# Another order of the first block's lists, and a query bound's small operations behind its maximum, in an attention and GEGLU block on one core

## The chip, the cores and the metric

The kernel runs on one core of a Trainium2 chip. The metric is the device time of one execution in microseconds (us), taken as the median of several runs. PE is the matrix engine (PEld its weight loads), ACT is ScalarE, DVE is VectorE, POOL is GpSimd and SP is SyncE, which issues most DMAs.

## The reference

One transformer block for a prompt of 2048 tokens of width 512, in float32: attention with 32 query heads of 16 columns that share one key and one value head, and then a GEGLU feed-forward of inner width 1792.

```python
def _A_ref(x, wq, wk, wv, wo):      # H = 32, Dh = 16
    q = (x @ wq).reshape(B, S, H, Dh).transpose(0, 2, 1, 3)
    k = x @ wk
    v = x @ wv
    scores = jnp.einsum("bhqd,bkd->bhqk", q, k) * (Dh ** -0.5)
    p = _softmax(scores, axis=-1)
    o = jnp.einsum("bhqk,bkd->bhqd", p, v)
    return o.transpose(0, 2, 1, 3).reshape(B, S, H * Dh) @ wo
def _B_ref(x, w_gate, w_up, w_down):
    return (_gelu(x @ w_gate) * (x @ w_up)) @ w_down
h = x + _A_ref(_layernorm(x), ...)
h2 = h + _B_ref(_layernorm(h), ...)
```

## The kernel before

The queries are cut into four blocks of 512 tokens. A block has eight groups of four heads, and a group runs over 16 chunks of 128 keys. The unit of attention is a *score pair* (`scores`, L352 and L356): two matmuls that write a PSUM tile of 128 keys x 1024, and one exponential of ScalarE over it into the tile p. Two pairs make a chunk; its V-product (`weigh`, L360) is a set of matmuls that add p's four heads into the accumulator acc. In the first block there are three PSUM tiles for score pairs (s twice, s3 once), one bank for the accumulator and one bank, "d", for everything else. A block has 256 pairs, counted here from 0, and 128 V-products.

A group's last V-product is followed by `evacuate`: DVE copies acc to oT (L373), SyncE writes oT to DRAM (`acc_d`, L374), and a later step reads it back turned (oc, four DMAs, L384). After every second group DVE takes reciprocals of the sums (L389), multiplies and splits the result into o_hi and o_lo. For the last group of block 0 all these steps are emitted at once. The first dense product, `project` (pp, L761), reads o_hi and o_lo.

A float32 product is made of three products of rounded parts, "hi" and "lo", so operands are split: `split` makes a rounded copy (L125) and the rest (L126).

The softmax needs no maxima: a bound of each query's scores, from the norms of q and k, is subtracted, as one more row of q. `project_q` makes the queries of a block in four column parts: twelve matmuls each into bank d (L205), the split, the squares qs, and three DMAs into `q_d`. Behind the four parts a small matmul adds the squares up by head (pqn, L243), DVE copies the result to qn (L247) and takes its maximum (L248), GpSimd makes scale and shift of it in four operations on 32 x 1 elements (mm, L252 to L259), DVE makes the row m (L270), and SyncE stores it (L272). The first column part of block 0 is made in the prologue with a bound of its own ("urgent"); the other three parts of block 0 and all of blocks 1 to 3 are made within the first block, as one generator, `later_q`. Its last step, `check_bound`, takes the largest bound and writes it to `b_d` with a DMA (L1363) from the tile q2m. `project_q` yields a number after each step, by which the caller counts.

The order in the first block is written out by hand as two lists of letters, `OPENING` once and `PERIOD` eight times (for eight groups). The letter s calls `pace`: one score pair, and after every fourth pair a step of turned outputs (`take_out`) and one part of the dense weights. The letter v is one V-product, p is a `visit` of the query generator, and n is `norm`, which runs the sums of squares if the last visit ended with a 4. A visit takes steps until their numbers add up to 6, or until a 2 comes. After the lists the pairs go on in a simple loop to pair 278, and then the woven lists of the dense phase begin.

The dense weights are split on GpSimd during the first block: `part_weights` has 46 parts, each a load, the split into a hi and a lo tile, and a store to DRAM (w_d, L460 and L466). At the end of the block the tiles of the queries and of these parts are given up (`early.close()`), and the tiles of the dense phase take their memory. `prime` issues the first nine loads into these: three of x (L519), three of the first weights (L501) and three of the second (L509). Where it stands is said by a count of pairs in `pace`:

```python
if n == 2 * PER:
    drain()
    ...
    early.close()
    db = late.enter_context(tc.tile_pool(name="dense", bufs=1))
...
score(n)
n += 1
...
if n == 2 * PER + 4:
    prime()
```

`PER` is 128. PE, ACT and POOL run in the order of emission in all of the attention, and SP and DVE do so in the first block's lists and the loops after it.

Of the kernel before, what the change touches and what calls it, by code (L numbers as in the profile page):

```python
# [29 lines left out]

HURRY = ((0, 3), (1, 0), (1, 1))

OPENING = "ssspsspsp"

PERIOD = "ssvssvssvnssvvsssvsvssvssvvssspssvvsssvvsspsssvvsnssp"

RUNS = ((0, 1, 2, 3), (4, 5, 6, 7), (8, 9, 10, 11), (12, 13))

# [19 lines left out]
def kernel(  # L58
# [62 lines left out]
    def split(eng_hi, hi, lo, src, eng_lo=None):  # L121
        if eng_hi is nc.scalar:
            nc.scalar.activation(hi, src, AF.Copy)
        else:
            eng_hi.tensor_copy(hi, src)  # L125
        (eng_lo or nc.vector).tensor_tensor(lo, src, hi.bitcast(F32), op=ALU.subtract)  # L126
# [29 lines left out]
    def run(outer, first):  # L156
# [10 lines left out]
        def psum1(name):  # L167
            if not spare:
                return ps.tile([P, T], F32, tag="d", bufs=width, name=name)
            tag, bank = take_bank(name)  # L170
            spare.append(tag)
            return bank
# [22 lines left out]
        def project_q(b, cs, eng, col):  # L195
            tsl = slice(b * T, (b + 1) * T)
            xT_hi, xT_lo = xT[b]
            urgent = b == 0 and cs[0] == 0
            qss = []
            for c in cs:  # L200
                pq = psum1(f"pq_{b}_{c}")
                n = 0
                for d in range(DC):
                    for wt, xt in ((wq_hi, xT_hi), (wq_hi, xT_lo), (wq_lo, xT_hi)):
                        nc.tensor.matmul(  # L205
                            pq, wt[:, d, c * P : (c + 1) * P], xt[:, d, :],
                            start=(n == 0), stop=(n == 3 * DC - 1),
                        )
                        n += 1
                    if urgent or d < DC - 1:  # L210
                        yield 3

                raw = None
                if (b, c) in HURRY:
                    raw = eb.tile([P, T], F32, tag="vT", bufs=3, name=f"pq_raw_{b}_{c}")
                    if b == 0:
                        nc.scalar.activation(raw, pq, AF.Copy)
                    else:
                        nc.vector.tensor_copy(raw, pq)
                    yield 3  # L220
                qh = eb.tile([P, T], F32R, tag="qh", bufs=2, name=f"qh_{b}_{c}")
                ql = eb.tile([P, T], F32R, tag="ql", bufs=2, name=f"ql_{b}_{c}")
                if raw is not None:
                    split(nc.vector, qh, ql, raw)
                else:

                    split(nc.vector if b == 0 and c == FIRST_Q else eng, qh, ql, pq)
                qs = eb.tile([P, T], BF16, tag="qs", bufs=DC, name=f"qs_{b}_{c}")
                (nc.gpsimd if urgent else nc.vector).tensor_tensor(
                    qs, qh.bitcast(F32), qh.bitcast(F32), op=ALU.mult  # L230
                )
                qss.append(qs)
                for r0, part in ((0, qh), (DH, ql), (2 * DH, qh)):
                    nc.sync.dma_start(
                        q_d[c * HC : (c + 1) * HC, r0 : r0 + DH, tsl].bitcast(F32),
                        part.bitcast(F32),
                    )
                if raw is None or b == 0:
                    yield 4 if b > 0 and c == DC - 1 else 3

            pn = psum1(f"pqn_{b}_{cs[0]}")[:H, :]
            for i, c in enumerate(cs):
                nc.tensor.matmul(  # L243
                    pn, sel[:, c, :], qss[i], start=(i == 0), stop=(i == len(cs) - 1)
                )
            qn = eb.tile([H, T], F32, tag="qn", bufs=1, name=f"qn_{b}_{cs[0]}")
            nc.vector.tensor_copy(qn, pn)  # L247
            nc.vector.tensor_reduce(q2[:, col : col + 1], qn, axis=AX.X, op=ALU.max)  # L248
            yield 2

            mm = eb.tile([H, 3], F32, tag="mm", bufs=2, name=f"mm_{b}_{cs[0]}")
            nc.gpsimd.tensor_scalar(  # L252
                mm[:, 0:1], q2[:, col : col + 1], k2m, 1e-30, op0=ALU.mult, op1=ALU.add
            )
            nc.gpsimd.tensor_tensor(mm[:, 1:2], mm[:, 0:1], power[:H, 0:1], op=ALU.pow)
            nc.gpsimd.tensor_scalar(
                mm[:, 2:3], mm[:, 0:1], mm[:, 1:2], 0.5, op0=ALU.mult, op1=ALU.mult
            )
            nc.gpsimd.tensor_scalar(  # L259
                mm[:, 1:2], mm[:, 1:2], k2m, 0.5, op0=ALU.mult, op1=ALU.mult  # L260
            )
            m = eb.tile([H, T], F32R, tag="m", bufs=2, name=f"m_{b}_{cs[0]}")
            if urgent:
                nc.scalar.activation(
                    m, qn, AF.Identity, bias=mm[:, 2:3], scale=mm[:, 1:2]
                )
                ms[b] = m
                return
            yield 0
            nc.vector.tensor_scalar(m, qn, mm[:, 1:2], mm[:, 2:3], op0=ALU.mult, op1=ALU.add)  # L270
            hs = slice(cs[0] * HC, (cs[-1] + 1) * HC)
            nc.sync.dma_start(q_d[hs, 3 * DH, tsl].bitcast(F32), m[hs].bitcast(F32))  # L272
            yield 2

        ms = {}
        q_first = project_q(0, range(FIRST_Q), nc.scalar, 0)
# [2 lines left out]
        def later_q():  # L279
            second = project_q(1, range(DC), nc.vector, 1)  # L280
            for _ in range(DC):
                yield next(second)

            next(q_rest)
            yield from q_rest
            yield from second
            for b in range(2, NB):
                yield from project_q(b, range(DC), nc.vector, b)
            check_bound(eb, k2m)
# [77 lines left out]
        def take_out():  # L367
            for step in outs.pop(0):
                step()
# [162 lines left out]
        def prime():  # L532
            new_xT(0)
            for i in range(3):
                load_x(i)
                load_w1(i)
            for j in range(3):
                load_w2(0, j)
# [405 lines left out]
        work = None  # L944
# [11 lines left out]
        def drain():  # L956
            nonlocal work
            for _ in work or ():
                pass
            work = None  # L960
# [30 lines left out]
        with tc.manual_schedule(engines={mybir.EngineType.SP, mybir.EngineType.DVE}):  # L991
            parts = None
            if first:
                work = later_q()
                parts = part_weights(early.enter_context(tc.tile_pool(name="parts", bufs=1)))


            normed = True

            def visit():  # L1000
                nonlocal work, normed
                total, k = 0, None
                while work is not None and total < 6 and (k != 2 or last == 0):
                    last, k = k, next(work, None)
                    if k is None:
                        work = None
                        return
                    total += k
                normed = k != 4

            def norm():
                nonlocal normed
                if not normed:
                    next(work)
                    normed = True

            def pace():
                nonlocal n, parts, db, tiny
                if n == 2 * PER:
                    drain()  # L1020
                    for _ in parts or ():
                        pass
                    parts = None
                    early.close()
                    db = late.enter_context(tc.tile_pool(name="dense", bufs=1))
                    tiny = late.enter_context(tc.tile_pool(name="tiny", bufs=1))
                score(n)
                n += 1
                if n % 4:
                    return  # L1030
                if outs:
                    take_out()
                if parts is not None and n > 12 and n % 24:
                    next(parts, None)
                if n == 2 * PER + 4:
                    prime()

            moves = {"s": pace, "p": visit, "n": norm, "v": partial(finish, 1)}
            for move in OPENING + PERIOD * (PER // KC):
                moves[move]()  # L1040
            while n < lead:
                pace()
                if n % 4 == 2 and len(pend) > 2 and n < lead - 1:
                    finish(1)
                elif n % 4 == 0:
                    finish(len(pend) - 2)
# [394 lines left out]
```

## Time and profile before

| | us |
|---|---|
| median of 3 runs | 1422.35 |
| lowest and highest | 1422.34, 1423.45 |
| the profiled execution | 1423.57 |
| its span, first to last instruction | 1421.5 |

The profiled execution lies about 2 us above its span and 1.2 us above the median. Its mean granted clock of TensorE was 0.995. Times within the profile count from the start of the span; the lists of the first block run from about 52 to 310 us. In a timeline's row stand the start, the length, the engine and line, the operation with its tiles, the count of merged instructions, and in brackets the idle time before it and what ended it. "SPq" is SyncE's queue.

### The profile page before, as it was taken

The numbers are of one execution on the slowest core, as the hardware profiler recorded it, in microseconds if no ns is written. First come the engines' busy times: TensorE is split into PE (matmuls) and PEld (weight loads), VectorE is DVE, ScalarE is ACT, GpSimd is POOL, SyncE is SP. The second block draws the span as 40 slices with busy tenths as digits, with TensorE's granted clock in tenths as the row PEclk, the third lists the DMA queues.
The fourth block names the chain that finished last, engine by engine and source line by source line (L and its number), as shares of the span: only waits on it lengthen the run. The fifth ranks groups of instructions, "written<-read, shape, count | busy, mean of one in ns | idle before, by whom it ended". The sixth has DMA issues, their size and how long they took to land.

```text
span 1421.5 us, 25079 instructions
## 1 busy us (share of the span) xinstructions
PE 1392.2 (98%) x10384; PEld 752.6 (53%) x10384; DVE 635.9 (45%) x1043; ACT 1030.0 (72%) x1147; POOL 217.0 (15%) x305
## 2 busy tenths in 40 slices
PE   6999999999999999999999999999999999999998
PEld 5433333335455555555555555545555555557886
DVE  7413121314364354454354444445354453437665
ACT  6699999997777777777777777777777777752000
POOL 5586776610000000000000000000000000001000
PEclk9999999999999999999999999999999999999999
DMA  4467666625222333322432333311332332244452
GB/s 158 138 200 247 211 222 212 222 98 201 73 88 94 116 101 116 101 65 57 156 102 86 127 105 101 104 61 42 141 105 90 116 116 101 90 148 174 126 189 77
DMA packets 66930, 180.57 MB, mean 127 GB/s; under 512 B 9436, under 2 KB 9436, under 8 KB 66776
## 3 DMA queue, kind: packets, MB, share of 16 engines
q1 hardware_dynamic: 56976, 144.79, 30.8%
q0 software_dynamic: 9760, 34.08, 7.3%
q8 instruction: 84, 1.38, 0.4%
q14 instruction: 38, 0.31, 0.1%
q10 hardware_dynamic: 72, 0.00, 0.0%
HBM read 131.13 MB, written 47.71 MB: 126 GB/s over the span
## 4 chain that ended last, share of the span: by engine, by line
PE 93%; ACT 2%; DVE 2%; DMA 1%; issue 1%; POOL 0%; SPq 0%; DVEq 0%; ACTq 0%; POOLq 0%
PE acc L360 32%; PE s L352 20%; PE pg L761 8%; PE pu L761 8%; PE pd L761 8%; PE pq L205 3%; PE pd L791 3%; PE pp L761 3%; PE pu L791 2%; PE pg L791 2%; ACT p L356 2%; PE pd_rest L803 1%; PE pxt L587 0%; DMA w<-w_d 0%; PE pk L1229 0%
## 5 line engine op out<-in xcount | busy, mean ns | idle before, releaser
L356 ACT ACTIVATE p<-s 128x1024 f32<-128x1024 f32 x1024 | 959.5, 1040 | 233.8 <-PE s L352 233.5
L360 PE MATMUL acc<-p,v_sb 128*32 128x512 f32 x4096 | 491.7, 600 | 0.0
L352 PE MATMUL s<-qg,kaug 50*128 50x512 f32 x1984 | 386.5, 426 | 4.0 <-ACT p L356 3.5
L352 PEld LDWEIGHTS s<-qg,kaug 50*128 50x128 f32 x1984 | 170.7, 184 | 288.2 <-issue 131.3
L360 PEld LDWEIGHTS acc<-p,v_sb 128*32 128x32 f32 x4096 | 110.4, 109 | 229.6 <-issue 216.1
L761 PE MATMUL pg<-x2h,w 64*128 64x512 f32 x672 | 173.9, 392 | 0.0
L761 PE MATMUL pu<-x2h,w 64*128 64x512 f32 x672 | 172.5, 391 | 0.0
L135 POOL TENSOR_SCALAR rstd<-mv 128x1 f32<-128x1 f32 x16 | 3.5, 220 | 968.0 <-DVE mv L133 967.8
L761 PE MATMUL pd<-w,gh 64*128 64x512 f32 x624 | 123.9, 392 | 1.4 <-DVE h L691 1.4
L691 DVE TENSOR_TENSOR h<-h,pd 128x512 f32<-128x512 f32 x80 | 54.4, 686 | 148.1 <-PE pd L761 148.1
L761 PEld LDWEIGHTS pg<-x2h,w 64*128 64x128 f32 x672 | 94.3, 185 | 11.5
L761 PEld LDWEIGHTS pu<-x2h,w 64*128 64x128 f32 x672 | 94.2, 185 | 11.5
L761 PE MATMUL pg<-x2l,w 64*128 64x512 f32 x336 | 99.2, 391 | 0.0
L761 PE MATMUL pu<-x2l,w 64*128 64x512 f32 x336 | 98.8, 391 | 0.0
L761 PEld LDWEIGHTS pd<-w,gh 64*128 64x128 f32 x624 | 68.3, 185 | 13.3 <-DVE h L691 2.7
L900 ACT ACTIVATE ga<-ga 128x512 f32<-128x512 f32 x14 | 8.8, 632 | 91.0 <-DVE ga L897 91.0
L389 DVE RECIPROCAL oc<-oc 128x128 f32<-128x128 f32 x64 | 56.6, 922 | 37.4 <-DMA oc<-acc_d 37.3
L761 PE MATMUL pd<-w,gl 64*128 64x512 f32 x312 | 71.7, 391 | 0.0
L628 DVE TENSOR_TENSOR g<-g,pg 128x512 f32<-128x512 f32 x42 | 28.8, 685 | 90.5 <-PE pg L761 90.5
L624 DVE COPY g<-pg 128x512 f32<-128x512 f32 x42 | 29.1, 692 | 72.1 <-PE pg L761 72.1
L628 DVE TENSOR_TENSOR u<-u,pu 128x512 f32<-128x512 f32 x42 | 28.8, 686 | 68.0 <-PE pu L761 68.0
L125 DVE CAST qh<-pq 128x512 fp32r<-128x512 f32 x11 | 7.6, 690 | 113.3 <-PE pq L205 113.3
(244 smaller groups left out, 1478.9 us busy)
## 6 DMA issues: line engine op xcount, KB each, us to landing
w<-w_d SPq DMA_DIRECT2D x112, 512.0 KB
w<-w_d SPq DMA_DIRECT2D x28, 1024.0 KB
qg<-q_d SPq DMA_DIRECT2D x62, 200.0 KB
q_d<-qh SPq DMA_DIRECT2D x32, 256.0 KB
acc_d<-oT SPq DMA_DIRECT2D x32, 256.0 KB
oc<-acc_d SPq DMA_DIRECT2D x128, 64.0 KB
w_d<-w_0b POOLq DMA_DIRECT2D x14, 512.0 KB, 4.1
w_d<-w_1b POOLq DMA_DIRECT2D x14, 512.0 KB, 3.8
```

The costliest lines, as they stand in the source:

```text
L205: nc.tensor.matmul(pq, wt[:, d, c * P : (c + 1) * P], xt[:, d, :], start=(n == 0), stop=(n == 3 * DC - 1),)
L352: nc.tensor.matmul(s[:, a, :], kaug[rows, kc * P : (kc + 1) * P], qg[rows, u, :], start=True, stop=True,)
L356: nc.scalar.activation(p[:, 2 * u : 2 * u + 2, :], s, AF.Exp, scale=SCALE)
L360: nc.tensor.matmul(acc[32 * j : 32 * j + 32, :], v_sb[:, kc, :], p[:, j, :], start=(kc == 0), stop=(kc == KC - 1), skip_group_check=True,)
L389: nc.vector.reciprocal(oc[:, 1, sl], oc[:, 1, sl])
L624: nc.vector.tensor_copy(half, bank)
L628: nc.vector.tensor_tensor(half, half, bank, op=ALU.add)
L691: nc.vector.tensor_tensor(hs[b, t], hs[b, t], bank, op=ALU.add)
L761: nc.tensor.matmul(bank, lhsT[r], rhs[r], start=(k == 0), stop=(k == n - 1), skip_group_check=True,)
L791: nc.tensor.matmul(bank, lhsT, rhs, start=(i == 0), stop=(i == len(ts) - 1))
L803: nc.tensor.matmul(bank, lhsT, rhs, start=(i == 0), stop=(i == len(ts) - 1))
L900: nc.scalar.activation(a, a, AF.Tanh, scale=GELU_A * GELU_C)
```

## The change

Three things are changed. `OPENING` and `PERIOD` get another order. For the queries other than the urgent ones, the yield of 2 that stood between the maximum and the four GpSimd operations moves behind these; the yield of 0 that stood ahead of m is gone, and the yield of 2 behind m's DMA is now 0. So the four operations are emitted in the same visit as the maximum, and m and its DMA remain at the start of the next visit. And `visit` no longer goes on behind a 2 that follows a 0: it ends at every 2.

```diff
-OPENING = "ssspsspsp"
-
-PERIOD = "ssvssvssvnssvvsssvsvssvssvvssspssvvsssvvsspsssvvsnssp"
+OPENING = "ssspssps"
+
+PERIOD = "psssvvssvnsspsssvvssvnssvssvssvvssspssvssvvnsssvvssvss"
...
             nc.vector.tensor_reduce(q2[:, col : col + 1], qn, axis=AX.X, op=ALU.max)
-            yield 2
-
+            if urgent:
+                yield 2
             mm = eb.tile([H, 3], F32, tag="mm", bufs=2, name=f"mm_{b}_{cs[0]}")
             nc.gpsimd.tensor_scalar(
                 mm[:, 0:1], q2[:, col : col + 1], k2m, 1e-30, op0=ALU.mult, op1=ALU.add
...
                 ms[b] = m
                 return
-            yield 0
+            yield 2
             nc.vector.tensor_scalar(m, qn, mm[:, 1:2], mm[:, 2:3], op0=ALU.mult, op1=ALU.add)
             hs = slice(cs[0] * HC, (cs[-1] + 1) * HC)
             nc.sync.dma_start(q_d[hs, 3 * DH, tsl].bitcast(F32), m[hs].bitcast(F32))
-            yield 2
+            yield 0
...
                 total, k = 0, None
-                while work is not None and total < 6 and (k != 2 or last == 0):
-                    last, k = k, next(work, None)
+                while work is not None and total < 6 and k != 2:
+                    k = next(work, None)
                     if k is None:
                         work = None
                         return
```

## The prediction

> **What bounds the kernel now.** I read the page first, then the chain of waits in the first block, then the timelines of PE, GpSimd, SyncE and DVE around the places where the two lists differ.
>
> ```profile
> span 1421.5 us, 25079 instructions
> PE 1392.2 (98%) x10384; PEld 752.6 (53%) x10384; DVE 635.9 (45%) x1043; ACT 1030.0 (72%) x1147; POOL 217.0 (15%) x305
> PE 93%; ACT 2%; DVE 2%; DMA 1%; issue 1%; POOL 0%; SPq 0%; DVEq 0%; ACTq 0%; POOLq 0%
> ```
>
> The chain that ends last is 93% PE: a microsecond in which PE stands still anywhere is, to within little, a microsecond of the kernel. The next view is the chain of waits from 68 to 300 us (the first block's lists) and some of its pieces from 151 to 184 us (start, length, engine, line, matmul records); the last row is one of ScalarE's timeline.
>
> ```profile
> by line: PE acc L360 48.7%; PE s L352 33.8%; PE pq L205 15.1%; ACT p L356 1.0%; PE pqn L243 0.8%; issue 0.4%; DVE qn L247 0.3%; ACTq L356 0.0%
> ...
> 162.11 1.85 PE acc L360 x16
> 163.97 0.89 PE s L352 x6
> 164.86 0.99 PE acc L360 x8
> ...
> 172.49 1.59 PE pq L205 x6
> 174.08 0.66 PE s L352 x3
> ...
> 71.25 7.44 ACT L356 ACTIVATE p<-s 128x1024 f32<-128x1024 f32 x8 [0.45 <-PE s L352]
> ```
>
> So the first block too is PE's: only 1.0 + 0.4 + 0.3 = 1.7% of 232 us, 3.9 us, is time in which PE waited. The pieces give prices: two V-products in a row 1.85, a single one 0.99, a run of three score pairs 0.89 and of two 0.66 (0.20 a run and 0.23 a pair), a projection visit of six matmuls 1.59. ScalarE takes (7.44 - 1.10) / 7 = 0.906 us a pair, the last one's 1.10 taken off.
>
> **The order of the lists.** I counted the letters of both periods. Each has 32 s, 16 v and 3 p, and, what matters for PE, the same runs: 14 of s, 11 of v (5 doubles, 6 singles), 3 of p. PE's own time in a period is 14 x 0.20 + 32 x 0.23 + 5 x 1.85 + 6 x 0.99 + 3 x 1.59 = 30.1 us in both, against 32 x 0.906 = 29.0 for ScalarE. The order can therefore give back only PE's waits, at most 3.9 us. The old gaps between visits are 19, 7 and 6 pairs, the new ones 7, 14 and 11. In a gap PE gains 0.906 - (0.66 + 0.99) / 2 = 0.08 us a pair on ScalarE and can spend it only as far as the three score tiles reach; 19 pairs gain 1.5, 14 pairs 1.1. I take a gain of 1.4 us (0.2 a period over seven full ones), between -1 (the product of block 1's squares is now followed by a projection after two pairs, as block 2's was) and 3.9. Opening, drain and the pairs after the lists stay as they were.
>
> **The small operations.** Four GpSimd operations (L252 to L259) now stand one visit earlier, behind their maximum; m on DVE and its DMA stay in the next visit. GpSimd runs its queue in order, and that queue is otherwise the splitting of the dense weights, 46 parts that wait for nothing in the attention. So a bound set early in that queue stops the splitting until DVE has the maximum. Here is GpSimd's timeline where the bound of block 1, of block 2 and of block 3 stand or will stand, with DVE's maximum of block 1 ahead:
>
> ```profile
> 131.41 0.67 DVE L248 TENSOR_REDUCE q<-qn 32x1 f32<-32x512 f32 x1
> ...
> 111.47 1.28 POOL L126 TENSOR_TENSOR w_1b<-w_1r,w_1b 128x512 fp32r<-128x512 f32 x1
> ...
> 132.00 1.28 POOL L126 TENSOR_TENSOR w23b<-w23r,w23b 128x512 fp32r<-128x512 f32 x1
> ...
> 134.94 0.74 POOL L466 DMA_DIRECT2D w_d<-w23b  x1
> ...
> 202.82 1.28 POOL L126 TENSOR_TENSOR w_1b<-w_1r,w_1b 128x512 fp32r<-128x512 f32 x1
> ...
> 211.66 1.28 POOL L126 TENSOR_TENSOR w_0b<-w_0r,w_0b 128x512 fp32r<-128x512 f32 x1
> ...
> 220.32 0.64 POOL L460 DMA_DIRECT2D w_d<-w_0b  x1 [0.63 <-issue]
> ...
> 291.39 0.63 POOL L466 DMA_DIRECT2D w_d<-w213b  x1 [0.30 <-POOL w213b L126]
> 306.84 0.25 POOL L252 TENSOR_SCALAR mm<-q,k2m 32x1 f32<-32x1 f32 x1 [14.83 <-DVE q L248]
> ```
>
> By the lists, block 1's bound moves from behind part 16 (w23b, done at 133.28) to behind part 12 (w_1b, done at 112.75). Its maximum ends at 132.08 now; in the new list it comes one pair earlier and about 1 us of order gain sooner, 130.8. So GpSimd stands still from 113 to 130.8, and the chain of four takes 1.6: 132.4. (The first bound, which now also stands ahead of the first weight loads, delays the first parts by some us; this stand swallows it.) Then parts 13 to 16 (112.75 to 133.28: 20.5), 17 to 30 (134.64 to 204.10: 69.5), block 2's bound now behind part 30 and no longer behind part 32 (1.6, its maximum long there), parts 31 and 32 (204.10 to 212.94: 8.8) and the rest (220.0 to 292.0: 72.0): 132.4 + 20.5 + 69.5 + 1.6 + 8.8 + 72.0 = 304.8. In those stretches are data waits of up to 5 us each that may fall differently; I take 303, between 299 and 308, where it is 292.0 now. DVE's m of block 2 then waits until about 224; behind it on DVE stands the split of the projection at pair 172 (about 219.5), whose bank PE needs again only at pair 186: free. On SyncE m's DMA holds back a turn of outputs that is not due before pair 220: free.
>
> **What the shifted end does.** In both kernels the dense phase's first nine loads (`prime`) are issued in the pace of pair 259, and the last group of block 0 is evacuated at V-product 127. In the old list that product stands between pairs 258 and 259, in the new one behind 259. SyncE keeps program order, so the nine loads now go ahead of the write and the turn of the last outputs. Today's rows, SyncE, then DVE, then PE:
>
> ```profile
> 309.05 0.35 SPq L272 DMA_DIRECT2D q_d<-m  x1
> 309.50 0.36 SPq L1363 DMA_DIRECT2D b_d<-q2m  x1
> 309.95 0.38 SPq L374 DMA_DIRECT2D acc_d<-oT  x1
> 316.86 1.92 SPq L384 DMA_DIRECT2D oc<-acc_d  x4
> 319.26 0.35 SPq L519 DMA_DIRECT2D xb<-in_A_x_dram  x1
> ...
> 322.03 2.75 SPq L509 DMA_DIRECT2D w<-w_d  x3
> 324.83 0.81 SPq L337 DMA_DIRECT2D qg<-q_d  x2
> ...
> 341.69 0.36 SPq L374 DMA_DIRECT2D acc_d<-oT  x1
> 343.83 1.47 SPq L384 DMA_DIRECT2D oc<-acc_d  x3
> ...
> 308.49 0.53 DVE L270 TENSOR_SCALAR m<-qn,mm 32x512 fp32r<-32x512 f32 x1 [1.76 <-POOL mm L259]
> ...
> 309.20 0.69 DVE L373 COPY oT<-acc 128x512 f32<-128x512 f32 x1
> 320.82 3.39 DVE L389 RECIPROCAL oc<-oc 128x128 f32<-128x128 f32 x4 [10.92 <-DMA oc<-acc_d]
> ...
> 325.43 0.69 DVE L126 TENSOR_TENSOR o_lo<-oc,o_hi 128x512 fp32r<-128x512 f32 x1
> ...
> 328.77 0.40 PE L761 MATMUL pp<-wo_hi,o_hi 64*128 64x512 f32 x1
> ```
>
> Today o is whole at 325.43 + 0.69 = 326.1, and PE wants it at 328.77: 2.7 us of slack. The new chain: the last bound starts when GpSimd is through, 303; b_d leaves 309.50 - 306.84 = 2.66 later, 305.7 (m and q2m are then off DVE before the last oT, due about 308). The loads reuse the memory of the first block's tiles and so wait for b_d's landing. No row shows that; writes of this kind took from 2.1 (341.69 to 343.83) to 6.9 us (309.95 to 316.86); I take 3.5, nearer to the undisturbed one. With 0.5 for SyncE's checks (318.78 to 319.26) the loads start at 309.7. They are 3 x (256 + 512 + 1024) KB = 5.5 MB. How long they take, and what an idle PE does to its clock, is in these stretches (width, busy us of PE, PEld, DVE, ACT, POOL, clock, DMA share, GB/s):
>
> ```profile
> 57.00:60.00 3.00, 1.41 (x6) 0.47 (x5) 2.32 (x4) 1.69 (x2) 0.00 (x0) 1.00 0.83 265
> 60.00:67.00 7.00, 7.00 (x29) 1.90 (x28) 1.35 (x2) 3.88 (x4) 4.34 (x5) 0.51 0.58 195
> ...
> 319.00:328.00 9.00, 8.59 (x64) 2.52 (x62) 5.20 (x7) 8.75 (x10) 0.00 (x0) 1.00 0.82 298
> 328.00:337.00 9.00, 9.00 (x72) 5.22 (x70) 0.69 (x1) 6.26 (x7) 0.00 (x0) 1.00 0.97 367
> ...
> SPq L374 <- DMA w<-w_d: 1.3, 1, 1.3
> ```
>
> The rings move 9 x 0.298 + 9 x 0.367 = 6.0 MB up to 337 (the loads, the end of the turn and two query loads), so the loads take about 17 us. The write of the last oT is issued when SyncE is through with nine issues (5.6 us) and lies behind them: it lands about 1 us after the last load, 309.7 + 17 + 1 = 327.7. Then turn and reciprocals as today: 320.82 - 316.86 = 3.96 and 326.12 - 320.82 = 5.30: o at 337.0, PE's first projection at 337.1 and not at 328.77. That is 8.3 us, and the order gain is inside it: PE only comes to the wait sooner. The Trainium skill (DMA: Bandwidth & Descriptors, Queues, rings and completion order) says that each engine consumes one issuer's descriptors in ring order; by that rule the write cannot pass the loads, and the last row above, a load that SyncE still waited for long after its issue, agrees.
>
> PE then stood idle for some 10 us. Where it was busy for less than half of 3 us (57 to 60), the next 7 us were granted a clock of 0.51. Half speed for 3.4 to 7 us costs 1.7 to 3.4; none at all costs 0; I take 2.5. The Trainium skill (TensorE: Matmul & The Clock Gate, Part 1) names windows of 3.4 us and half the clock after an idle one; by it the price is an estimated 1.7 or more, which leaves the sum as it is.
>
> **Sum.** 8.3 + 2.5 = 10.8 us. The profiled execution was 1423.57 us with a span of 1421.5; it lies 1.2 above the median of 1422.35. Its successor would have a span of 1432.3; on the median, 1433.2. The mechanism's own range: GpSimd's end 299 to 308 (-4, +5), b_d's landing (-1.4, +3.4), the clock (-2.5, +1), taken together as independent: 1428 to 1439.
>
> **Rivals.** (1) *The write is not held*: the rings serve it beside the loads. SyncE issues it at 315.3, it lands 2.1 us later at 317.4, o is whole at 326.7, before PE is there (328.77 - 1.4 = 327.4). Only the order gain is left: 1421.0, faster than before, up to 1418.5 if all waits go. It decides from the point where the write lands before 318.1. For it: the write has 256 KB only. Against it: the load that landed late. The same comes out if GpSimd is through by about 294 and the loads are over when oT is ready. Chance 0.12. (2) *All cancels*: the chain slips by no more than its slack of 2.7 and what the order gains, and the run counts being equal nothing else changes: 1422.4. Chance 0.06. (3) *GpSimd is later still*: from an end at 306 on, m holds DVE beyond the last oT, the accumulator's bank comes free late as well, and each us counts in full: 1440 and more. Chance 0.07.
>
> **How the numbers follow.** My forecast has 0.75. Its range holds nine tenths of it; to hold 8 in 10 I reach down to rival 1, 1421, and to 1439. This kernel's measurement tells some 0.2% (2.8 us) from no change. Slower by that: the forecast and rival 3, less the forecast's low tail, 0.81. Within: rival 2, most of rival 1 and that tail, 0.15. Faster: the rest of rival 1, 0.04.
>
> **What would show it.** Right: GpSimd idle before the bound of block 1 for 13 to 18 us, released by DVE; its last part after 299; SyncE's xb and w loads ahead of the last acc_d write of block 0, oc some 20 us later than that write's copy; a wait of PE of about 10 us for o at the first projection, with the clock at half behind it; the lists themselves 1 to 2 us shorter. Wrong: no wait of PE at L761 near 330, or the loads behind the oc turns as today.

## The result, and the profile after

The changed kernel is slower by 0.5 to 0.6%: a median of 1429.44 us in 5 runs (1427.92 to 1432.67) against 1422.34 in 5 runs of the kernel before on the same chip, which is 7.1 us; the ratio on record is 1.0057 (0.57%, or 8.1 us), 95% interval 1.0044 to 1.0071. Predicted were 1433.2 us, between 1421 and 1439. The profiled execution took 1432.67 us and is the slowest of its five: it lies 3.2 above their median, where that of the kernel before lay 1.2 above its own. The page of the profile, its first lines and the chain by engine:

```profile
span 1430.8 us, 25077 instructions
PE 1391.4 (97%) x10384; PEld 753.2 (53%) x10384; DVE 634.6 (44%) x1043; ACT 1030.6 (72%) x1147; POOL 218.3 (15%) x305
PE 92%; DMA 3%; ACT 1%; DVE 1%; issue 1%; SPq 0%; POOL 0%; DVEq 0%; ACTq 0%
```

PE's busy time hardly differs (1392.2 before), and the span is 9.3 longer: PE stood still. In the chain DMA has gone from 1% to 3%. The chain of waits from 280 to 345 us (start, length, what) shows where these transfers stand:

```profile
308.48 0.35 SPq L519
...
314.96 13.27 DMA acc_d<-oT
...
329.56 2.30 DMA oc<-acc_d
...
331.98 3.40 DVE oc L389 x4
...
336.13 0.44 DVE o_hi L125
...
336.70 1.22 PE pp L761 x4
```

It is the chain that the prediction described: the loads of the dense phase (from L519), the write of the last oT behind them, its turn, the reciprocals, the split, and only then the first projection. The timelines of GpSimd, SyncE, DVE and PE around it:

```profile
117.58 1.28 POOL L126 TENSOR_TENSOR w_1b<-w_1r,w_1b 128x512 fp32r<-128x512 f32 x1
128.66 0.26 POOL L252 TENSOR_SCALAR mm<-q,k2m 32x1 f32<-32x1 f32 x1 [9.79 <-ACT p L356]
...
301.51 0.26 POOL L252 TENSOR_SCALAR mm<-q,k2m 32x1 f32<-32x1 f32 x1
...
304.19 0.34 SPq L1363 DMA_DIRECT2D b_d<-q2m  x1
308.48 0.35 SPq L519 DMA_DIRECT2D xb<-in_A_x_dram  x1
...
313.00 1.51 SPq L509 DMA_DIRECT2D w<-w_d  x3
314.96 0.33 SPq L374 DMA_DIRECT2D acc_d<-oT  x1
328.25 1.73 SPq L384 DMA_DIRECT2D oc<-acc_d  x4
...
288.65 0.67 DVE L248 TENSOR_REDUCE q<-qn 32x1 f32<-32x512 f32 x1
...
303.17 0.53 DVE L270 TENSOR_SCALAR m<-qn,mm 32x512 fp32r<-32x512 f32 x1 [13.84 <-POOL mm L259]
304.92 0.69 DVE L373 COPY oT<-acc 128x512 f32<-128x512 f32 x1 [0.97 <-PE acc L360]
...
336.59 0.69 DVE L126 TENSOR_TENSOR o_lo<-oc,o_hi 128x512 fp32r<-128x512 f32 x1
...
324.38 0.39 PE L761 MATMUL pp<-wo_hi,o_hi 64*128 64x512 f32 x1
...
326.68 0.40 PE L761 MATMUL pp<-wo_hi,o_lo 64*128 64x512 f32 x2
336.70 0.79 PE L761 MATMUL pp<-wo_hi,o_hi 64*128 64x512 f32 x2 [9.62 <-DVE o_hi L125]
...
338.28 4.60 PE L360 MATMUL acc<-p,v_sb 128*32 128x512 f32 x24
```

GpSimd stands still for 9.8 us before block 1's bound; the row names ScalarE as what ended it, but DVE's maximum, done at 128.5, is what the bound reads. oT is copied by 305.61, but SyncE issues its write only at 314.96, behind nine loads, and the write takes 13.3 us until the turn can start; before it was issued at 309.95 and took 6.9. The maximum of the last bound is done at 289.3 now, long before GpSimd is through with the weights (301.5), where it came at 306.7 before, after them. PE starts the first projection at 324.38, runs the terms of the earlier column parts, and stops for the last part of o. Two views more, the waits from 300 to 345 us and the stretches (width, busy us of PE, PEld, DVE, ACT and POOL, clock, DMA share, GB/s):

```profile
DVE oc L389 <- DMA oc<-acc_d: 26.4, 1, 26.4
...
PE pp L761 <- DVE o_hi L125: 9.6, 1, 9.6
```

```profile
308.00:313.00 5.00, 5.00 (x44) 1.46 (x40) 0.00 (x0) 4.81 (x6) 0.00 (x0) 1.00 0.51 100
...
318.00:323.00 5.00, 4.59 (x38) 1.58 (x40) 0.00 (x0) 5.00 (x6) 0.00 (x0) 1.00 1.02 416
...
331.70:336.70 5.00, 0.00 (x0) 0.03 (x1) 4.61 (x7) 0.00 (x0) 0.00 (x0) 0.51 0.20 63
336.70:342.00 5.30, 5.29 (x26) 1.85 (x30) 0.59 (x1) 1.02 (x1) 0.00 (x0) 0.50 0.00 0
342.00:346.00 4.00, 4.00 (x34) 2.52 (x28) 1.18 (x2) 2.59 (x3) 0.00 (x0) 1.00 0.00 0
```

The granted clock falls to half some 5 us into the idle stretch and stays there for 5.3 us of PE's work, which so takes 2.6 longer.

The account of the first block, by the starts of ScalarE's exponentials in the two profiles: pair 300 starts at 365.46 and not at 357.72, 7.7 later. Pair 16 starts 2.3 earlier (70.80, 73.08), since the profile of before was at half clock from 60.1 to 66.9 and that of after was not; the 262 pairs from 16 to 278 take 251.39 and not 253.48, 2.1 less; the wait is 9.6 and the half clock 2.6: -2.3 - 2.1 + 9.6 + 2.6 = 7.8. The last 1.5 of the 9.3 come after pair 300. From there to the end the kernels of this document do the same work, and in their 14 profiles this stretch took 1061.9 to 1065.4 us; it is 1063.8 in the profile of before and 1065.4, the longest of all, in that of after. So these 1.5 us are no more than executions differ by.

### The profile page after: what moved, and what is told of

Read it like the earlier page. It is cut to its first block, busy times and chain, and to the rows that moved or that the text cites. A ratio compares the mean times of both kernels' runs of the same rounds, so it can differ in the third digit from the quotient of the medians.

```text
span 1430.8 us, 25077 instructions
## 1 busy us (share of the span) xinstructions
PE 1391.4 (97%) x10384; PEld 753.2 (53%) x10384; DVE 634.6 (44%) x1043; ACT 1030.6 (72%) x1147; POOL 218.3 (15%) x305
## 4 chain that ended last, share of the span: by engine, by line
PE 92%; DMA 3%; ACT 1%; DVE 1%; issue 1%; SPq 0%; POOL 0%; DVEq 0%; ACTq 0%
PE acc L360 32%; PE s L352 20%; PE pg L761 8%; PE pu L761 8%; PE pd L761 8%; PE pq L205 4%; PE pd L791 3%; PE pu L791 2%; PE pg L791 2%; PE pp L761 2%; DMA acc_d<-oT 1%; DMA w<-w_d 1%; ACT p L356 1%; PE pk L1229 1%; PE pd_rest L803 1%
## 5 line engine op out<-in xcount | busy, mean ns | idle before, releaser
L761 PEld LDWEIGHTS pu<-x2h,w 64*128 64x128 f32 x672 | 94.7, 186 | 11.2
L373 DVE COPY oT<-acc 128x512 f32<-128x512 f32 x32 | 22.1, 691 | 111.1 <-PE acc L360 110.9
```

What stands on the lines that cost most here:

```text
L373: nc.vector.tensor_copy(oT, acc)
L761: nc.tensor.matmul(bank, lhsT[r], rhs[r], start=(k == 0), stop=(k == n - 1), skip_group_check=True,)
```

## The experiments

The theory is the prediction's: the time is lost because SyncE issues the nine loads ahead of the last group's write, and the order of the lists does that. The rivals are that the place of the small operations matters by itself, that the write is late for another reason than the loads, and that GpSimd's late end is the root.

**The loads behind the write again.** The changed kernel, with `prime` four pairs later:

```diff
-                if n == 2 * PER + 4:
+                if n == 2 * PER + 8:
                     prime()
```

> The changed kernel with the nine loads issued in the pace of pair 263 and no longer of 259, so that they stand behind the last group's write and turn again. Queue theory (the loss is PE's wait for o, and the write lies behind the loads): the wait at L761 near 327 us is gone, what is left is the lists' gain, 1419 to 1421.5 us. Lists theory (the new order or GpSimd's earlier stand costs the time by itself): 1427 or more, as the changed kernel.

Measured: 1420.04 us, ratio to the kernel before 0.9979 [0.9969, 0.9989]. Its timeline of SyncE:

```profile
305.90 0.37 SPq L374 DMA_DIRECT2D acc_d<-oT  x1
312.27 1.71 SPq L384 DMA_DIRECT2D oc<-acc_d  x4
...
315.15 0.35 SPq L519 DMA_DIRECT2D xb<-in_A_x_dram  x1
```

The write goes 9.1 us sooner and takes 6.4; PE has no wait at the projection. GpSimd's last bound is as late (302.78), so a late end of GpSimd alone costs nothing. All that the changed kernel loses comes from SyncE's order, and what is left is a gain.

**The loads ahead of the write in the old kernel.** Nothing of the change, only its side effect:

```diff
                     tiny = late.enter_context(tc.tile_pool(name="tiny", bufs=1))
+                    prime()
...
-                if n == 2 * PER + 4:
-                    prime()
```

> The kernel before, lists and yields untouched, with the nine loads issued at the drain, ahead of the last group's evacuation. Queue theory: the loads wait for b_d (about 313 us), the write lies behind them, o comes at about 341 and not 326, and PE waits 12 us and then runs at half clock for a while: 1434 to 1437 us. Lists theory: no lists were changed, so 1422.

Measured: 1434.32 us, ratio 1.008 [1.0065, 1.0095]. SyncE's timeline and the wait:

```profile
306.66 0.37 SPq L1362 DMA_DIRECT2D b_d<-q2m  x1
310.47 0.35 SPq L519 DMA_DIRECT2D xb<-in_A_x_dram  x1
...
316.87 0.45 SPq L374 DMA_DIRECT2D acc_d<-oT  x1
330.32 1.74 SPq L384 DMA_DIRECT2D oc<-acc_d  x4
```

```profile
PE pp L761 <- DVE o_hi L125: 10.1, 1, 10.1
```

The loss is there in full without the change, and the wait, 10.1, is 2 us below what was expected. GpSimd's last store stood at 287.89 here; its last bound waited for DVE's late maximum, as in the kernel before. So a late end of GpSimd isn't needed for the loss either, and the loads may be held by the one or the other.

**The old lists with the small operations moved**, and **the new lists with the small operations at their old place** (there with the loads behind the write, as in the first experiment), each with the rule of `visit` that belongs to its yields; the edit is that of the first:

```diff
-OPENING = "ssspssps"
+OPENING = "ssspsspsp"
-PERIOD = "psssvvssvnsspsssvvssvnssvssvssvvssspssvssvvnsssvvssvss"
+PERIOD = "ssvssvssvnssvvsssvsvssvssvvssspssvvsssvvsspsssvvsnssp"
```

> The old lists with the small operations behind the maximum. Queue theory: the loads stand where they stood, GpSimd's stand is swallowed: 1421 to 1424 us. If the earlier small operations cost by themselves (DVE or GpSimd held up): 1425 or more.

> The new lists with the old place of the small operations, and the loads in the pace of pair 263. Queue theory: the same as with the new place, within 1 us, 1419 to 1421.5 us, since the small operations are on nobody's path. If the small operations' new place is what brings a gain: slower than that kernel by over 1 us.

Measured: 1423.27 us, ratio 1.0003 [0.9994, 1.0013], and 1418.81, ratio 0.9981 [0.9972, 0.9989], the same as 0.9979 with the small operations moved. With the old lists SyncE's order is the old one (write at 308.64, loads from 317.55). So the lists alone bring the gain, and the place of the small operations is worth nothing that can be measured. That the lists alone bring the loss too follows from the order of SyncE's queue that they give; they were not run with the old yields and the loads at their own place. Pairs 16 to 278 took 251.40 in the first experiment and 251.43 in this last one, and 253.45 in the second: 2.0 to 2.1 us belong to the lists.

**Fewer bytes ahead of the write.** The changed kernel, with the three second-weight loads of 1024 KB moved out of `prime` to four pairs later:

```diff
+                if n == 2 * PER + 8:
+                    for j in range(3):
+                        load_w2(0, j)
```

> The changed kernel with six loads (2.4 MB) left ahead of the write and the three largest (3.1 MB) issued four pairs later, behind it. Ring theory (the write waits for the bytes ahead of it): it lands at 316 to 318 us and not at 328, o comes before or with PE, 1419 to 1423 us. Issue theory (the write is late because it is issued late and shares the engines, whatever lies ahead): it still takes some 13 us from its issue, PE waits about 8 us, 1427 to 1429.

Measured: 1421.21 us, ratio 0.9989 [0.9976, 1.0003]. Timeline of SyncE and the wait:

```profile
314.50 0.43 SPq L374 DMA_DIRECT2D acc_d<-oT  x1
321.86 1.72 SPq L384 DMA_DIRECT2D oc<-acc_d  x4
```

```profile
PE pp L759 <- DVE o_hi L125: 2.4, 1, 2.4
```

The write is issued as late as in the changed kernel, but takes 7.4 and not 13.3 us. So two things are lost in its place in the queue: about 9 us until it is issued (305.90 with the write ahead), and 6 while it lies behind the last 3 MB. It landed later than I had written, and a wait of 2.4 us stayed; the profiled execution, 1425.6 us, is also one of the three slowest of the eleven, the other eight of which lie between 1418.6 and 1421.4.

The 6.4 us with none ahead are no measure of the write alone. In that run its bytes have moved by 307.7, and from there to 312.2 no queue of the core starts a packet (in the kernel before, none from 311.8 to 316.8); what the turn waits for in this time stays open. A write of the same size with nothing around it takes 2.1 us (349.51 to 351.64 in the changed kernel). Against this the loads ahead cost 5.3 us here, where 1.8 of the 2.4 MB were still to move when the write was issued, and 11.2 in the changed kernel, where 4.2 of the 5.5 were.

What the write does behind the loads can be read from the packets. A load of the weights moves in packets of 4 KB, the write in 128 packets of 2 KB. The changed kernel's packets from 317 to 325 us (packets, MB; for a queue the share of 16 engines' time behind them), while the write had been issued at 314.96:

```profile
DMA packets 848, 3.29 MB, mean 411 GB/s; under 512 B 49, under 2 KB 49, under 8 KB 847
q1 hardware_dynamic: 847, 3.27, 101.8%
```

The 847 packets of SyncE's queue (q1) less the 49 smallest are 798, and 3.27 MB are just 798 times 4 KB: in these 8 us the write did not move at all. It was held until the loads ahead of it were through.

**The write by another engine.** The changed kernel, with the last group's write and turn issued by GpSimd, which is idle by then:

```diff
-            nc.sync.dma_start(acc_d[:, g % 4, :], oT)
+            eng = nc.gpsimd if b == 0 and g == NG - 1 else nc.sync
+            eng.dma_start(acc_d[:, g % 4, :], oT)
...
-                    nc.sync.dma_start(oc[r0 : r0 + DH, :, :], view[j])
+                    eng.dma_start(oc[r0 : r0 + DH, :, :], view[j])
```

> The changed kernel with the last group's write and turn of block 0 issued by GpSimd, which has nothing else to do by then; the loads stay where they are on SyncE. Queue theory (it is the place behind nine loads in SyncE's queue): the write leaves at 306 us, o is there before PE wants it, 1418 to 1421.5. If the loads hold the write up through the shared engines wherever it is issued: a wait of some us stays, 1424 to 1429.

Measured: 1418.32 us, ratio 0.9976 [0.9967, 0.9985]. GpSimd's timeline:

```profile
306.95 0.62 POOL L375 DMA_DIRECT2D acc_d<-oT  x1 [3.96 <-DVE oT L373]
312.51 2.04 POOL L385 DMA_DIRECT2D oc<-acc_d  x4 [4.95 <-DMA acc_d<-oT]
```

The loads stand where they stand in the changed kernel (from 308.27), and PE doesn't wait. The turn, though, now runs beside 5.5 MB of loads: from the end of its issue at 314.55 to the reciprocals at 321.66 are 7.1 us, where the changed kernel needs 2.0 behind them. The write itself took 5.6 us, but it was issued 1.3 us ahead of the loads, so it is the turn that shows what a queue of its own is worth. The packets of the two queues from 316 to 321 us:

```profile
q1 hardware_dynamic: 325, 1.09, 81.1%
q0 software_dynamic: 128, 0.26, 24.2%
```

The turn's 256 KB on GpSimd's queue (q0) move among the loads of SyncE's: on its own queue a small transfer is slowed, but not held. The Trainium skill (DMA: Bandwidth & Descriptors, Queues, rings and completion order) has each DMA engine consume descriptors in ring order and makes each queue row a ring of its own there; the trace agrees, with the write held behind 5.5 MB on SyncE's queue and the turn served beside them from GpSimd's.

**The changed kernel again, and the landing that the loads wait for.** The second has q2m, the source of b_d's write, in a pool that isn't given up; it ran on another chip (the two that ran beside the first are the write by GpSimd and the second run on GpSimd's end):

```diff
-        q2m = sb.tile([H, 1], F32, name="q2m")
+        q2m = const.tile([H, 1], F32, name="q2m")
```

> The changed kernel itself, beside the next two on the same chip: 1428 to 1431 us.

> The changed kernel with the tile q2m, from which b_d is written, outside of the memory that the loads reuse. If b_d's landing starts the loads: they start when m has landed, 305 to 306 us and not 308.5, and the time falls by 2 to 3.5 us, to 1426 to 1427.5. If not: 1429 to 1430.

Measured: 1429.54 us, ratio 1.0052 [1.0038, 1.0065], and 1427.2, ratio 1.0048 [1.0032, 1.0063]. From b_d's issue to the first load are 4.0 us in the repeat (303.13 to 307.15) and 2.0 with the other pool (304.51 to 306.48). So the loads do wait for the landing of that small write, about 2 us of it. But the issue of the second load ended at 309.2 and 310.2, no sooner with the other pool, and the turns start at 327.52 and 327.77; PE's wait is 9.4 and 8.0. The time gains at most the 2 us, within the scatter of the runs, and the ratios are the same, so that 1427.2 lies in the expected range proves little.

**GpSimd's end.** Four runs tried to bring it back; each is the changed kernel with another rule for the steps of the weights (one added line a run, the remarks behind # are mine). GpSimd's "stand" is its idle time in front of a bound:

```diff
-                if parts is not None and n > 12 and n % 24:
+                if parts is not None and n > 12:                                # no step left out
+                if parts is not None and n > 12 and (n % 24 or n in (48, 72)):  # two more steps
+                if parts is not None and n > 20 and n % 24:                     # and two at n == 4
+                if parts is not None and n > 12 and n % 24:                     # and two at n == 4
```

> The changed kernel with one part of the dense weights after every fourth pair without the pauses at every 24th, so that more parts stand ahead of block 1's bound and GpSimd has less time in which it stands still. GpSimd theory (the loads start when GpSimd's last bound has reached b_d): GpSimd ends at 291 to 296 us, the loads start at 299 to 303 and not at 308.5, o comes 6 to 9 us sooner, 1420 to 1424 us. If something else starts the loads: 1428 to 1430.

> The changed kernel with two of the paused parts (at pairs 48 and 72) given back: 14 and no longer 12 parts stand ahead of block 1's bound, so that GpSimd works through most of its stand, and reaches block 2's bound at the same time as in the changed kernel. GpSimd theory (its end starts the loads): GpSimd's last part ends at 291 to 295 us and not at 301.4, the loads start at 299 to 302, o comes 6 to 9 us sooner and PE waits 0 to 3 us: 1419 to 1424. If something else starts the loads: 1428 to 1431.

> The changed kernel, with the two first parts of the weights emitted at pair 4, ahead of block 0's bound, instead of at pairs 16 and 20; from pair 24 on as many parts are emitted as in the changed kernel. In the changed kernel GpSimd's first store stands at 85.35 and not at 80.26, its seventh at 115.77 and not at 107.26. Theory (the end of GpSimd is set by the stand before block 1's bound, which takes up whatever was lost or gained ahead of it): first store 80 to 81, seventh 107 to 111, the stand before the bound of block 1 14 to 19 us instead of 9.8, GpSimd's last store 299 to 302 as in the changed kernel, PE's wait for o 8 to 10 us, 1427 to 1431. Rival (the late first parts are what makes GpSimd's end late): last store 293 to 297, the loads start at 300 to 304, PE's wait 2 to 6 us, 1421 to 1425.

> The changed kernel, with two parts of the weights emitted at pair 4, ahead of block 0's bound, besides those that it emits later; so each later bound has two more parts ahead of it. Theory (GpSimd's end follows from both bounds: the run with two more parts ahead of block 1's bound had no stand there any more, and kept the late first parts): first store 80 to 81, a stand of 3 to 10 us before block 1's bound, last store 291 to 296, the loads start 5 to 8 us sooner than in the changed kernel, PE's wait for o 1 to 5 us, 1420 to 1425. Rival (GpSimd's own loads set its end, whatever stands before the bounds): last store 299 to 301, as in the run with two more parts, PE's wait 8 to 10, 1427 to 1431.

Measured, in this order: 1435.27 us, ratio 1.0095 [1.0079, 1.011]; 1429.57, 1.0057 [1.0043, 1.0071]; 1429.14, 1.0046 [1.0029, 1.0063]; 1426.69, 1.0024 [0.9999, 1.0048], the ten runs of the last from 1417.49 to 1432.84.

The first shows the prediction's third rival, in an earlier block: with every step taken, block 2's bound stands behind too many parts, m holds DVE, the split behind m holds bank d, and PE waits (the waits, from 55 to 350 us):

```profile
DVE m L270 <- POOL mm L259: 45.7, 4, 31.3
...
PE pq L205 <- DVE ql L126: 15.7, 1, 15.7
```

The second took nearly all of the stand before block 1's bound away:

```profile
128.40 0.26 POOL L252 TENSOR_SCALAR mm<-q,k2m 32x1 f32<-32x1 f32 x1 [0.70 <-ACT p L356]
```

and yet GpSimd's last store stood at 299.85, against 300.79 in the changed kernel. That was a miss, and it showed me a part that I had left out. In the changed kernel the first bound stands ahead of the first weight loads, so GpSimd's first store of weights is at 85.35 and not at 80.26, its seventh at 115.77 and not at 107.26: of the 9.4 us by which its last store is late, 5.1 are there at the first store and 8.5 at the seventh, before the stand begins. The third run puts the first two parts ahead of that bound (first store 80.57, seventh 112.78): the stand grew to 11.9 us and the last store stayed at 300.46, as the theory has it, though seventh store and stand lie outside of what was expected (107 to 111, 14 to 19). The fourth has both; the stand shrank to 5.2, and its profile still has the last store at 301.13, against the theory. GpSimd's waits in that profile, from 60 to 310 us, and those of the kernel before:

```profile
POOL w_1b L125 <- DMA w_1r<-in_B_w_up_dram: 22.3, 9, 5.1
...
POOL w28r L455 <- DMA w28r<-in_B_w_down_dram: 5.9, 1, 5.9
POOL mm L252 <- ACT p L356: 5.2, 1, 5.2
POOL w24r L455 <- DMA w24r<-in_B_w_down_dram: 4.9, 1, 4.9
```

```profile
POOL w_1b L125 <- DMA w_1r<-in_B_w_up_dram: 19.6, 11, 4.6
...
POOL w213r L455 <- DMA w213r<-in_B_w_down_dram: 5.5, 1, 5.5
```

There GpSimd waited more for its own loads, and what a bound no longer took they did. The sums of these waits from 60 to 305 us say so for all these profiles: for loads and bounds 37 and 16 us in the changed kernel, 46 and 7 in the second of the four runs, 41 and 12 in the third, 52 and 5 in the fourth; in the kernel before they are 42 and 5. Three of the ten runs (1417.49, 1418.0, 1421.01) were about as fast as the kernels in which PE doesn't wait, the other seven took 1425.8 to 1432.8; no trace shows a fast one. Their granted clocks, 0.997 and 0.998 against 0.993 to 0.996 in the other seven, fit executions without PE's long wait; that GpSimd was through sooner in them is only likely. In the twelve kernels with the new lists, the moved operations or both, the last store stood at 299.8 to 302.9; in the two with neither at 287.9 and 291.4. Either half of the change is enough for the later end (the old lists with the moved operations 301.28, the new lists with the old ones 300.47). Why the loads then take what a bound gives back stays open.

## Why the prediction was right, and where it was off

**Order of the lists.** Predicted 1.4 us, measured 2.1 (253.48 to 251.39, and the same in three other kernels): right, and the term was 0.7 too small. That PE's work is equal and only its waits can be saved held.

**GpSimd.** Predicted an end between 299 and 308, taken as 303; the last bound started at 301.51. The end was right, but not the way to it: the stand before block 1's bound is 9.8 and not 17.8, since its start was 117.6 + 1.3 and not 113 and the maximum came at 128.5 and not 130.8. I had written that the delay of the first parts is swallowed by the stand; at the seventh store it was 8.5 us, nearly as large as the stand. And with that stand taken away (0.7 us left) the last store came at 299.85 all the same. So the stand is not shown to be what makes the end late, and that the number agreed is in part luck. That the last maximum would be waiting was assumed and held (289.3).

**SyncE's queue.** Predicted, then measured: b_d leaves at 305.7, 304.19; the loads start at 309.7, 308.48; so b_d's landing and SyncE's checks took 4.3 where I had 4.0. The write was put behind nine issues, 315.3, and stood at 314.96; the turn could start at 327.7 by the sum and did at 328.25; o at 337.0, and was at 336.59 + 0.69 = 337.3; PE at 337.1, and it was 336.70, since the first matmuls of the last part need o_hi alone. The loads' first 5 us moved only 100 GB/s, so they took longer than the 17 us by about as much as they had started sooner. The first rival, a write that isn't held, is refuted: it moved nothing from 317 to 325, and took 13.3 us behind all the loads and 7.4 behind the smaller six. The row that I put up against this rival was misread: SyncE's wait before 341.69 ended with DVE's copy of oT (340.97 + 0.69), and a load that lands late would not show that a write cannot pass it.

**The wait.** I had counted 8.3 us from the first projection's old start, with the order gain inside; the wait is 9.6. PE was not stopped at its first projection, as I had it: it did the terms of the earlier column parts until 327.

**The clock.** Predicted 2.5 for some 10 us of idle time, measured 2.6 (half clock from about 331.7 to 342.0). The Trainium skill (TensorE: Matmul & The Clock Gate, Part 1) has windows of 3.4 us; the 10.2 us are three of them, so the trace agrees.

**The sum.** In the profile the terms come to 9.6 + 2.6 - 2.1 = 10.1 us, against 10.8 predicted. The span grew by 9.3: the half clock early in the profile of before takes 2.3 off, and the stretch from pair 300 on adds 1.5. On the medians it is 7.1, and 8.2 in the repeat. The weak step is the last one, which took the difference of two executions over to medians as if each lay alike among its kernel's runs; that of after lies 3.2 above its median, that of before 1.2. The early half clock does not explain this. It belongs to the execution and not to the kernel (6.8 us in the profile of before, none in that of after; of the twelve profiles of the experiments six had none and six had 3.4), but it made the profile of before the longer one, and so the difference of the profiles smaller. On one chip the changed kernel took 1429.54 and the one with the write on GpSimd 1418.32, so wait and clock together are worth 11.2 us of the medians, where the trace has 12.2; and the kernels that keep the lists without the wait lie 2.5 to 3.0 below the kernel before, where the trace has 2.1. That leaves some 8 us. Why both terms differ by up to a us from the trace was not measured.

The best version tried is the new order of pairs with the last group's write ahead of the loads or off their queue: 1418.3 to 1420.0, 0.2% below the kernel before.

## What to carry to other kernels

When an order written by hand is changed, look first at what two queues that share an emission count will do to each other: here the lists kept every engine's work and saved 2 us, but a V-product slid past a pair that triggers nine loads, and that cost 12. A small write that somebody waits for belongs ahead of megabytes of prefetch on its queue, or on another engine's queue; its price is the issue time of what stands ahead and the bytes that are still to go. And check each stand of a queue that you remove by where the queue ends, not by whether the stand is gone.

## What was not expected of the hardware

The write behind the loads: 13.3 us with 5.5 MB ahead and 7.4 with 2.4 MB, against 2.1 with nothing around it; not one of its packets moved in 8 us while loads of the same queue were being served. With none ahead it still took 6.4 us, of which 4.5 passed without a new packet on any queue. A DMA of one column of 32 values held the reuse of memory by loads that have nothing to do with it for 2 us. The half clock early in the kernel came and went between executions (6.8, 3.4 or 0 us). And one kernel, the last of the four on GpSimd's end, scattered over 15 us where the kernel before scattered over 4 on the same chip. SyncE's second load took 2.16 us to issue where the next ones took 0.42 (308.88 and 311.09), and little moved meanwhile; an instruction packet of 8 KB on queue q14 was in flight at the time (308.72 to 310.90), but that SyncE waited for it was not shown.
